# Transposing the exponential's rows as they are, and applying each head's reciprocal sum to its projected output

## The chip, the cores and the metric

The kernel runs on one core of one Trainium2 chip. The metric is device time in microseconds (us), the median of three runs; lower is better. The engines are named as the profile names them: PE is the tensor engine (matrix products), PEld its weight loads, ACT the scalar engine (exponentials), DVE the vector engine, POOL the gpsimd engine and SP the sync engine, which here issues most of the transfers. SBUF is the core's on-chip memory, PSUM the small memory that PE writes its products to.

## The reference

A block with two halves shares one conditioning vector. The first half, where the change lies, is attention of 2048 query rows over a cache of 2048 keys, with 32 query heads in 8 groups of 4 heads that share one key and value head:

```python
q = (h @ wq).reshape(B, Sq, 32, 128).transpose(0, 2, 1, 3)
scores = einsum('bhqd,bhkd->bhqk', q, k) * 128 ** -0.5      # k, v repeated 4 times per key head
p = softmax(scores, axis=-1)
o = einsum('bhqk,bhkd->bhqd', p, v)
x = x + ga * (o.transpose(0, 2, 1, 3).reshape(B, Sq, 4096) @ wo)
h = layernorm(x) * (1 + cb) + sb                            # then the second half
```

The second half is a gated spatial mixing block: `z = gelu(h @ w_in)`, the half `z2` of it normalised per row, multiplied from the left by a 2048 by 2048 matrix, a bias added, multiplied by the half `z1`, and projected by `w_out`. Data is bfloat16, sums are float32.

## The kernel before

**Units and iterations.** Work is cut into 128 units `u`: key head `g = u // 16` and query tile `j = u % 16` of 128 rows, with the 4 heads of the group in one unit. The main loop (L1373) has one iteration `it` for each unit and six more at the end; each has 8 slots `i`. The order of instructions on every engine is the order in which this loop writes them (a manual schedule): in each slot first what was put down for it with `at(it, slot, fn)`, then the scores and the exponential of unit `it` (`qk`), a share of the product with V of an earlier unit (`pv_part`), the query projection of a later block (`fill`), and at most one step of an output projection (`wo_proj`). From iteration 128 on each slot also takes three matmuls of the second half (`zrun(3)`).

**Two kinds of unit.** `by_rows(u)` is true for the even units from 8 to 124, 59 in all. In the other units the scores are computed with keys on the partitions, so the exponential comes out in the layout that the product with V needs; the row sums come from a column of ones beside V, and `pv` divides by them with a reciprocal and a multiplication (L1091, L1092) on a 128 by 256 piece. In a row unit the scores have queries on the partitions (L1005), ACT writes the exponential into a row buffer `pn` (the page names such a buffer `win_sb`, `wmod_a` or `pn`, since they share memory) and gives the sum of each half row (L1012). One head takes two slots. Two slots after its last exponential was written down, `turn_rows` adds the two half sums (L1045), takes the reciprocal into `rall` (L1048), multiplies the 128 by 2048 rows by it in place (L1050), and has a transfer of SP turn them (L1051). The product with V follows three iterations later (`pv_rows`, L1059), one 128 by 512 bank for four heads, which DVE copies to `oT` (L1068).

**Output projection.** `wo_proj(u)` makes four steps, one per head. Before, all four add up in one PSUM bank named `misc` (L1112), and DVE adds the bank to the unit's running sum `xacc` in SBUF (L1125; for the first key head it copies it, L1123). There are two `misc` banks, handed out in turn, and a matmul that opens a bank waits until DVE has read what stood there two turns earlier; the query projection (L945, read by DVE in L956) takes banks from the same two. For the last key head (units 112 to 127) four more DVE operations follow in a row: times `ga` (L1130), plus `x` (L1131), and the statistics of the second layer norm (L697, L698). I call these four the closing steps.

**Where the steps of a projection stand.** `wo_at(u)` puts the projection of a row unit 6 iterations after `u`, and that of another unit 4 after it; for units from 122 on it is one less. With four steps these take slots 4 to 7. Two iterations hold two projections, and there the eight steps fill slots 0 to 7: iteration 126 (units 120 and 123) and iteration 129 (units 124 and 126). In both the row unit comes first.

**The end.** After the last closing steps come, through `ln2`, one normalised tile each (L686), a transfer that turns it (L1149) and a scaling (L1156), then on DVE the statistics of `z2` (L1312, L1313) and its normalisation, which the spatial matmuls (L1456) read.

Of the kernel before, what the change touches and what calls it, by code (L numbers as in the profile page):

```python
# [11 lines left out]
FP32 = mybir.dt.float32  # L12
ACT = mybir.ActivationFunctionType
ALU = mybir.AluOpType
AX = mybir.AxisListType
P = 128
# [559 lines left out]
def kernel(  # L576
# [19 lines left out]
    nc = tc.nc  # L596
    _, S, D = A_x.shape
    _, HKV, SK, DH = A_k_cache.shape
    HQ = A_wq.shape[1] // DH
    REP = HQ // HKV  # L600
# [12 lines left out]
    NSLOT = NKT // 2  # L613
# [30 lines left out]
    late = free_b.enter_context(tc.tile_pool(name="late", bufs=2, side="right"))  # L644
    early = free_a.enter_context(tc.tile_pool(name="early", bufs=2))

    x_sb = res.tile([P, NT, D], BF16, name="x_sb")
    ga_rows = res.tile([P, D], FP32, name="ga_rows")
    gb_rows = res.tile([P, D], FP32, name="gb_rows")
    modc = res.tile([P, 6 * NDT], FP32, name="modc")  # L650
    rall = res.tile([P, NT * HQ], FP32, name="rall")
    mv1 = res.tile([P, NT, nc.vector.BN_AGGR_DIM], FP32, name="mv1")
    mv2 = res.tile([P, NT, nc.vector.BN_AGGR_DIM], FP32, name="mv2")
# [6 lines left out]
    pn = [win_t[:, r * SK : (r + 1) * SK] for r in range(REP - 1)]  # L660
# [34 lines left out]
    def ln_stats(mv, j, src):  # L695
        st = stat.tile([P, 1, nc.vector.BN_STATS_DIM], FP32, name="bnst")
        nc.vector.bn_stats(out=st[:, 0, :], in_=src)  # L697
        nc.vector.bn_aggr(out=mv[:, j, :], in_=st[:])  # L698
# [201 lines left out]
    for k in range(2):  # L900
        for dt in (2 * k, 2 * k + 1):
# [3 lines left out]
            else:  # L905
                nc.scalar.activation(
                    out=dst,
                    in_=src,
                    func=ACT.Identity,
                    scale=modc[:, NDT + dt : NDT + dt + 1],  # L910
# [52 lines left out]
    NU = HKV * NT  # L963


    TURN_A, TURN_B = 2 * CT, NU - 2

    def by_rows(u):
        return TURN_A <= u < TURN_B and u % 2 == 0

    def pv_at(u):
        return u + 3 if by_rows(u) else u + 1

    def wo_at(u):
        return pv_at(u) + (3 if u < TURN_B - CT else 2)
# [11 lines left out]
    def at(it, slot, fn):  # L987
        later.setdefault((it, slot), []).append(fn)

    def qk(u, i):  # L990
        g, j = divmod(u, NT)
        b, jj = g * NCH + j // CT, j % CT
        if i == 0:
            if homes[u] == "wsp":
                pTs[u] = wspp.tile([P, NT, 512], BF16, name="wsp")
            else:
                pTs[u] = late.tile([P, NKT, 512], BF16, name=homes[u], bufs=1)
            if by_rows(u):
                rsums[u] = stat.tile([P, NSLOT], FP32, name="rs")
        s_ps = bank2()  # L1000
        if by_rows(u):
            hh, half = divmod(i, 2)
            for c in range(2):
                k0 = (2 * half + c) * 512
                nc.tensor.matmul(  # L1005
                    s_ps[:, c * 512 : (c + 1) * 512],
                    lhsT=qTs[b][:, hh, jj * P : (jj + 1) * P],
                    rhs=groups[g]["kT"][:, k0 : k0 + 512],
                    start=True,
                    stop=True,  # L1010
                )
            nc.scalar.activation(  # L1012
                out=rows_of(u, hh)[:, half * HK : (half + 1) * HK],
                in_=s_ps[:],
                func=ACT.Exp,
                scale=inv_sqrt_dh,
                accum_out=rsums[u][:, i : i + 1],
            )
            if half == 1:
                at(*divmod(u * NSLOT + i + 2, NSLOT), lambda: turn_rows(u, hh))  # L1020
            return
        for h in range(2):
            kt = 2 * i + h
            nc.tensor.matmul(  # L1024
                s_ps[:, h * 512 : (h + 1) * 512].rearrange("p (r q) -> p r q", r=REP),
                lhsT=groups[g]["kT"][:, kt * P : (kt + 1) * P],
                rhs=qTs[b][:, :, jj * P : (jj + 1) * P],
                start=True,
                stop=True,
            )  # L1030
        nc.scalar.activation(  # L1031
            out=pTs[u][:, 2 * i : 2 * i + 2, :],
            in_=s_ps[:].rearrange("p (k q) -> p k q", k=2),
            func=ACT.Exp,
            scale=inv_sqrt_dh,
        )

    def rows_of(u, hh):
        return pn[((u - TURN_A) // 2 * REP + hh) % len(pn)][:, 0:SK]

    def turn_rows(u, hh):
        c0 = u * REP + hh
        rs, rinv = rsums[u], rall[:, c0 : c0 + 1]
        tot = stat.tile([P, 1], FP32, name="tot")
        nc.vector.tensor_tensor(  # L1045
            out=tot[:], in0=rs[:, 2 * hh : 2 * hh + 1], in1=rs[:, 2 * hh + 1 : 2 * hh + 2], op=ALU.add
        )
        nc.vector.reciprocal(out=rinv, in_=tot[:])  # L1048
        rows = rows_of(u, hh)
        nc.vector.tensor_scalar(out=rows, in0=rows, scalar1=rinv, scalar2=None, op0=ALU.mult)  # L1050
        nc.sync.dma_start_transpose(out=pTs[u][:, :, hh * P : (hh + 1) * P], in_=rows)  # L1051

    def pv_rows(u, i, n):

# [48 lines left out]

    def wo_proj(u):
        g, j = divmod(u, NT)
        ps = {}

        def mm(hh):
            if hh == 0:
                ps[0] = bank("misc")  # L1110
            X_ps = ps[0]
            nc.tensor.matmul(  # L1112
                X_ps[:],
                lhsT=oTs[u][:, hh, :],
                rhs=groups[g]["wo"][:, hh, :],
                start=(hh == 0),
                stop=(hh == REP - 1),
            )
            if hh < REP - 1:
                return  # L1120
            if g == 0:
                xaccs[j] = late.tile([P, D], FP32, name=f"xacc{j}", bufs=1)
                nc.vector.tensor_copy(out=xaccs[j][:], in_=X_ps[:])  # L1123
            else:
                nc.vector.tensor_tensor(  # L1125
                    out=xaccs[j][:], in0=X_ps[:], in1=xaccs[j][:], op=ALU.add
                )
            if g == HKV - 1:
                xa = xaccs[j]
                nc.vector.tensor_tensor(out=xa[:], in0=xa[:], in1=ga_rows[:], op=ALU.mult)  # L1130
                nc.vector.tensor_tensor(  # L1131
                    out=x_sb[:, j, :], in0=xa[:], in1=x_sb[:, j, :], op=ALU.add
                )
                ln_stats(mv2, j, x_sb[:, j, :])

        return [lambda hh=hh: mm(hh) for hh in range(REP)]

# [127 lines left out]
    for g in range(1, HKV):  # L1265
        it = (g - 1) * NT
        at(it + 11, 5, lambda g=g: load_k(g))
        loads = (
            lambda g=g: load_v(g),
            lambda g=g: load_wq(g, nc.gpsimd),  # L1270
            lambda g=g: load_wo(g, nc.gpsimd),
        )
        for k, load in enumerate(loads):
            if g == 1:
                at(5, 0, load)
                continue
            u = next(u for u in range(it + 4 + 2 * k, NU) if by_rows(u))
            at(u + 1, 5, lambda u=u: after_rows(u))
            at(u + 1, 5, load)

# [92 lines left out]
    for it in range(NU + 6):  # L1373
        if it < NU:
            if it % CT == 0 and it // CT + 1 < NB:
                set_fill(it // CT + 1)
        elif it == NU:
            free_a.close()
            z2p = fast.enter_context(tc.tile_pool(name="z2p", bufs=1))
            zs["z2"] = z2p.tile([P, NT, FH], BF16, name="z2")  # L1380
        pvs = [u for u in (it - 5, it - 3, it - 1) if 0 <= u < NU and pv_at(u) == it]
        wos = [u for u in range(max(it - 6, 0), min(it - 2, NU)) if wo_at(u) == it]
        wf = [fn for u in wos for fn in wo_proj(u)]
        for i in range(NSLOT):
            for fn in later.pop((it, i), []):
                fn()
            if it < NU:
                qk(it, i)
            if len(pvs) == 1:
                pv_part(pvs[0], i, NSLOT)  # L1390
            elif pvs:
                n = NSLOT // 2
                pv_part(pvs[i // n], i % n, n)
            for fn in fill.pop((it, i), []):
                fn()
            if i >= NSLOT - len(wf):
                wf[i - NSLOT + len(wf)]()
            if it >= NU:
                zrun(3)
        for u in wos:  # L1400
            if u >= (HKV - 1) * NT:
                ln2(it, u % NT)
        if it == NU + 2:
            free_b.close()
            mlp = fast.enter_context(tc.tile_pool(name="mlp", bufs=1, side="right"))
            zs["z1T"] = mlp.tile([P, NFT, S], BF16, name="z1T")
            wout_sb = mlp.tile([P, NFT, D], BF16, name="wout_sb")
            bsp_bc = mlp.tile([P, S], BF16, name="bsp_bc")
            nc.gpsimd.dma_start(out=wout_sb[:], in_=wout_dram)
            nc.gpsimd.dma_start(out=bsp_bc[:], in_=B_b_sp.partition_broadcast(P))  # L1410
# [165 lines left out]
```

## Time and profile before

| what | us |
|---|---|
| median of 3 runs (lowest, highest) | 1313.21 (1313.07, 1313.99) |
| span of the profiled execution, first to last instruction | 1311.5 |
| PE busy | 1303.8 |
| ACT busy | 1113.0 |
| DVE busy | 689.5 |
| POOL busy | 59.4 |
| rows times the reciprocal (L1050), 236 operations | 177.9 |
| bank added to `xacc` (L1125), 112 operations, and copied (L1123), 16 | 76.2 and 10.9 |

The page and the answers of the trace list, for each group of instructions, its line, engine and operation, the tile written and the tiles read, the shapes, the count, the busy time and the mean of one in nanoseconds, and after a bar the time that the engine stood idle just before them with what ended it. In a timeline the first two numbers are the start and the length in us, both on the span's clock. A matmul's length there includes the time in which its result travels; the next one starts earlier.

### The profile page before, as it was taken

Reading aid. Unit: us, or ns where it says so; the run is one execution under the profiler, and the core shown is the slowest. Engines: PE = TensorE matmul, PEld = TensorE weight load, DVE = VectorE, ACT = ScalarE, POOL = GpSimd, SP = SyncE. Lnnn points to the kernel's source line nnn. Section 1 sums busy time; section 2 is a strip of 40 time slices with the busy share of each in tenths; the row PEclk is TensorE's granted clock in tenths of the full one; section 3 lists DMA queues with packets and bytes.
Section 4 is the critical chain, followed back from the end, with each engine's and each line's share of the span. In section 5 each row is a group of like instructions: output and inputs, shape, how many; then the busy total and the mean of one; then the engine's idle time right before and its main releaser. Section 6 shows DMA issues by size and latency. Waiting matters only on the chain.

```text
span 1311.5 us, 24369 instructions
## 1 busy us (share of the span) xinstructions
PE 1303.8 (99%) x9527; PEld 736.9 (56%) x9527; DVE 689.5 (53%) x1693; ACT 1113.0 (85%) x1533; POOL 59.4 (5%) x115
## 2 busy tenths in 40 slices
PE   9999999999999999999999999999999999999998
PEld 5665555555555555555555555555555555644445
DVE  5644455444454544444445454444445588784444
ACT  7899999999999999999999999999999999550000
POOL 1200000000000000000000000000000011120000
PEclk9999999999999999999999999999999999999999
DMA  6669778877897677867886778668876688364300
GB/s 181 154 97 157 130 128 154 158 118 133 158 166 149 121 144 155 144 125 140 160 169 122 133 157 156 125 127 153 175 143 125 118 140 144 103 133 96 82 21 27
DMA packets 607723, 174.45 MB, mean 133 GB/s; under 512 B 597264, under 2 KB 603664, under 8 KB 607600
## 3 DMA queue, kind: packets, MB, share of 16 engines
q1 hardware_dynamic: 600576, 153.67, 64.9%
q0 software_dynamic: 4432, 16.91, 4.1%
q10 hardware_dynamic: 2592, 2.23, 0.5%
q8 instruction: 77, 1.26, 0.4%
q14 instruction: 46, 0.38, 0.1%
HBM read 21.89 MB, written 2.10 MB: 18 GB/s over the span
## 4 chain that ended last, share of the span: by engine, by line
PE 96%; DVE 2%; DMA 1%; POOL 0%; issue 0%; ACT 0%; DVEq 0%; POOLq 0%
PE o_ps L1080 19%; PE s_ps L1024 18%; PE s_ps L1005 16%; PE o_ps L1059 16%; PE misc L1112 8%; PE misc L945 8%; PE misc L1456 7%; PE s_ps L1290 1%; PE o_ps L1477 1%; DVE stz L1312 1%; PE s_ps L1477 1%; DMA xnT<-xn 0%; DMA wmod_a<-in_w_mod_dram 0%; DVE z L686 0%; POOL rstd_lnz L682 0%; PE misc L855 0%
## 5 line engine op out<-in xcount | busy, mean ns | idle before, releaser
L1031 ACT ACTIVATE pT<-s_ps 128x1024 bf16<-128x1024 f32 x552 | 561.1, 1025 | 30.7 <-PE s_ps L1024 8.7
L1080 PEld LDWEIGHTS <-pT 128*128 128x128 bf16 x4416 | 295.3, 98 | 128.9
L1080 PE MATMUL o_ps<-v,pT 128*128 128x129 bf16 x4416 | 339.7, 220 | 0.0
L1024 PE MATMUL s_ps<-qT,kT 128*128 128x512 bf16 x1104 | 328.1, 379 | 0.3 <-ACT pT L1031 0.2
L1005 PE MATMUL s_ps<-kT,qT 128*128 128x512 bf16 x944 | 280.7, 379 | 0.0
L1012 ACT ACTIVATE win_sb<-s_ps 128x1024 bf16<-128x1024 f32 x238 | 243.7, 1025 | 3.5
L1112 PE MATMUL misc<-wo_g,oT 128*128 128x512 bf16 x512 | 194.0, 379 | 0.0
L945 PE MATMUL misc<-hT,wq_g 128*128 128x512 bf16 (+2 forms) x520 | 187.0, 371 | 0.1
L1024 PEld LDWEIGHTS <-kT 128*128 128x128 bf16 x1104 | 107.3, 98 | 114.9 <-issue 2.3
L1012 ACT ACTIVATE pn<-s_ps 128x1024 bf16<-128x1024 f32 x156 | 159.6, 1024 | 2.0 <-ACT wmod_a L1012 0.3
L1059 PEld LDWEIGHTS <-v 128*128 128x128 bf16 x944 | 92.4, 98 | 111.4
L956 DVE CAST qT<-misc 128x512 bf16<-128x512 f32 x125 | 85.7, 686 | 122.8 <-PE misc L945 122.8
L1068 DVE CAST oT<-o_ps 128x512 bf16<-128x512 f32 x59 | 40.8, 692 | 194.9 <-PE o_ps L1059 194.9
L1059 PE MATMUL o_ps<-wsp,v 128*128 128x512 bf16 x480 | 142.1, 379 | 0.0
L1059 PE MATMUL o_ps<-pT,v 128*128 128x512 bf16 x464 | 138.0, 379 | 0.0
L1005 PEld LDWEIGHTS <-qT 128*128 128x128 bf16 x944 | 92.2, 98 | 61.6
L1045 DVE TENSOR_TENSOR tot<-rs 128x1 f32<-128x1 f32 x236 | 36.4, 154 | 127.1 <-ACT win_sb L1012 84.8
L1456 PE MATMUL misc<-wsp,z 128*128 128x512 bf16 (+2 forms) x560 | 101.4, 336 | 0.2
L1050 DVE TENSOR_SCALAR win_sb<-win_sb,rall 128x2048 bf16<-128x2048 bf16 x119 | 89.7, 753 | 4.4 <-DVE rall L1048 0.3
L1012 ACT ACTIVATE wmod_a<-s_ps 128x1024 bf16<-128x1024 f32 x78 | 79.9, 1025 | 0.0
L1456 PEld LDWEIGHTS <-z 128*128 128x128 bf16 x560 | 50.5, 98 | 49.4 <-DVE z L686 1.6
L1125 DVE TENSOR_TENSOR xacc<-misc,xacc 128x512 f32<-128x512 f32 x112 | 76.2, 680 | 0.0
(110 smaller groups left out, 824.1 us busy)
## 6 DMA issues: line engine op xcount, KB each, us to landing
v<-in_A_v_cache_dram POOLq DMA_DIRECT2D x7, 512.0 KB, 6.6
wq_g<-in_A_wq_dram POOLq DMA_DIRECT2D x7, 512.0 KB, 3.9
wo_g<-in_A_wo_dram POOLq DMA_DIRECT2D x7, 512.0 KB, 4.5
wsp<-in_w_mod_dram POOLq DMA_DIRECT2D x1, 2048.0 KB, 9.1
out_dram<-yout ACTq DMA_DIRECT2D x16, 128.0 KB, 1.7
win_sb<-in_B_w_in_dram POOLq DMA_DIRECT2D x1, 1792.0 KB, 8.0
x_sb<-in_A_x_dram SPq DMA_DIRECT2D x3, 512.0 KB, 6.1
oT<-onorm SPq DMA_TRANSPOSE x69, 2.8
```

The costliest lines, as they stand in the source:

```text
L945: nc.tensor.matmul(ps[0][:, o0 : o0 + n], lhsT=wqs[g][:, dt, hh * DH : (hh + 1) * DH], rhs=hTs[ch][:, dt, c0 : c0 + n], start=(dt == 0), s ...
L956: nc.vector.tensor_copy(out=dst, in_=src)
L1005: nc.tensor.matmul(s_ps[:, c * 512 : (c + 1) * 512], lhsT=qTs[b][:, hh, jj * P : (jj + 1) * P], rhs=groups[g]["kT"][:, k0 : k0 + 512], sta ...
L1012: nc.scalar.activation(out=rows_of(u, hh)[:, half * HK : (half + 1) * HK], in_=s_ps[:], func=ACT.Exp, scale=inv_sqrt_dh, accum_out=rsums[u ...
L1024: nc.tensor.matmul(s_ps[:, h * 512 : (h + 1) * 512].rearrange("p (r q) -> p r q", r=REP), lhsT=groups[g]["kT"][:, kt * P : (kt + 1) * P], ...
L1031: nc.scalar.activation(out=pTs[u][:, 2 * i : 2 * i + 2, :], in_=s_ps[:].rearrange("p (k q) -> p k q", k=2), func=ACT.Exp, scale=inv_sqrt_dh,)
L1050: nc.vector.tensor_scalar(out=rows, in0=rows, scalar1=rinv, scalar2=None, op0=ALU.mult)
L1059: nc.tensor.matmul(o_pss[u][:], lhsT=groups[g]["v1"][:, kt, 0:DH], rhs=pTs[u][:, kt, :], start=(kt == 0), stop=(kt == NKT - 1),)
L1080: nc.tensor.matmul(o_ps[:, hh % 2, 0 : DH + 1], lhsT=pTs[u][:, kt, hh * P : (hh + 1) * P], rhs=groups[g]["v1"][:, kt, 0 : DH + 1], start=( ...
L1112: nc.tensor.matmul(X_ps[:], lhsT=oTs[u][:, hh, :], rhs=groups[g]["wo"][:, hh, :], start=(hh == 0), stop=(hh == REP - 1),)
L1125: nc.vector.tensor_tensor(out=xaccs[j][:], in0=X_ps[:], in1=xaccs[j][:], op=ALU.add)
L1456: nc.tensor.matmul(g_ps[:, :n], lhsT=z2[:, st, f * P : (f + 1) * P], rhs=wsp[t][:, st, c0 : c0 + n], start=(st == 0), stop=(st == NT - 1 a ...
```

## The change

In a row unit the rows are no longer multiplied by the reciprocal. `turn_rows` issues the transposing transfer first, straight from the exponential, one slot earlier than before, and then adds the half sums and takes the reciprocal as before. The product with V is then short of the factor, and so is `oT`. `wo_proj` makes up for it: for a row unit each head's step opens a bank of its own, and DVE multiplies the bank by the head's column of `rall` while it adds it to `xacc`. Units that are not row units keep one bank and one addition. The order in which units, lags and buffers are chosen is written in another form and comes out the same.

```diff
     def turn_rows(u, hh):
         c0 = u * REP + hh
-        rs, rinv = rsums[u], rall[:, c0 : c0 + 1]
+        rs = rsums[u]
+        nc.sync.dma_start_transpose(
+            out=pTs[u][:, :, hh * P : (hh + 1) * P], in_=rows_of(u, hh)
+        )
         tot = stat.tile([P, 1], FP32, name="tot")
         nc.vector.tensor_tensor(
             out=tot[:], in0=rs[:, 2 * hh : 2 * hh + 1], in1=rs[:, 2 * hh + 1 : 2 * hh + 2], op=ALU.add
         )
-        nc.vector.reciprocal(out=rinv, in_=tot[:])
-        rows = rows_of(u, hh)
-        nc.vector.tensor_scalar(out=rows, in0=rows, scalar1=rinv, scalar2=None, op0=ALU.mult)
-        nc.sync.dma_start_transpose(out=pTs[u][:, :, hh * P : (hh + 1) * P], in_=rows)
+        nc.vector.reciprocal(out=rall[:, c0 : c0 + 1], in_=tot[:])
...
             if half == 1:
-                at(*divmod(u * NSLOT + i + 2, NSLOT), lambda: turn_rows(u, hh))
+                at(*divmod(u * NSLOT + i + 1, NSLOT), lambda: turn_rows(u, hh))
...
     def wo_proj(u):
         g, j = divmod(u, NT)
+        each = by_rows(u)
         ps = {}
 
+        def into(first, X_ps, scale):
+            if first:
+                xaccs[j] = late.tile([P, D], FP32, name=f"xacc{j}", bufs=1)
+            xa = xaccs[j]
+            if scale is None and first:
+                nc.vector.tensor_copy(out=xa[:], in_=X_ps[:])
+            elif scale is None:
+                nc.vector.tensor_tensor(out=xa[:], in0=X_ps[:], in1=xa[:], op=ALU.add)
+            elif first:
+                nc.vector.tensor_scalar(
+                    out=xa[:], in0=X_ps[:], scalar1=scale, scalar2=None, op0=ALU.mult
+                )
+            else:
+                nc.vector.scalar_tensor_tensor(
+                    out=xa[:], in0=X_ps[:], scalar=scale, in1=xa[:], op0=ALU.mult, op1=ALU.add
+                )
+
         def mm(hh):
-            if hh == 0:
+            if hh == 0 or each:
                 ps[0] = bank("misc")
...
             nc.tensor.matmul(
...
-                start=(hh == 0),
-                stop=(hh == REP - 1),
+                start=(hh == 0 or each),
+                stop=(hh == REP - 1 or each),
             )
+            if each:
+                c0 = u * REP + hh
+                into(g == 0 and hh == 0, ps[0], rall[:, c0 : c0 + 1])
+            elif hh == REP - 1:
+                into(g == 0, ps[0], None)
-            if hh < REP - 1:
+            if hh < REP - 1 or g < HKV - 1:
                 return
...
```

The closing steps for the last key head are unchanged. In the built program PE, ACT, POOL and SP carry the same instructions in the same order as before; on DVE 236 multiplications of rows go and 177 operations on banks come.

More of the change, by code (lines that the diff above doesn't have):

```diff
@@ L966 @@
     TURN_A, TURN_B = 2 * CT, NU - 2
+    LAGS = (3, 1)
     def by_rows(u):
-        return TURN_A <= u < TURN_B and u % 2 == 0
+        return TURN_A <= u < TURN_B and (u - TURN_A) % len(LAGS) < len(LAGS) - 1
+    row_units = [u for u in range(NU) if by_rows(u)]
     def pv_at(u):
-        return u + 3 if by_rows(u) else u + 1
+        return u + (LAGS[(u - TURN_A) % len(LAGS)] if by_rows(u) else 1)
     def wo_at(u):
@@ L1038, in rows_of @@
     def rows_of(u, hh):
-        return pn[((u - TURN_A) // 2 * REP + hh) % len(pn)][:, 0:SK]
+        return pn[(row_units.index(u) * REP + hh) % len(pn)][:, 0:SK]
     def turn_rows(u, hh):
         c0 = u * REP + hh
-        rs, rinv = rsums[u], rall[:, c0 : c0 + 1]
+        rs = rsums[u]
+        nc.sync.dma_start_transpose(
+            out=pTs[u][:, :, hh * P : (hh + 1) * P], in_=rows_of(u, hh)
+        )
         tot = stat.tile([P, 1], FP32, name="tot")
@@ L1108, in mm @@
         def mm(hh):
-            if hh == 0:
+            if hh == 0 or each:
                 ps[0] = bank("misc")
-            X_ps = ps[0]
             nc.tensor.matmul(
-                X_ps[:],
+                ps[0][:],
                 lhsT=oTs[u][:, hh, :],
                 rhs=groups[g]["wo"][:, hh, :],
-                start=(hh == 0),
-                stop=(hh == REP - 1),
-            )
-            if hh < REP - 1:
-                return
[L1121 to L1134, printed above, removed]
+                start=(hh == 0 or each),
+                stop=(hh == REP - 1 or each),
+            )
+            if each:
[3 more added lines that the diff above has]
+                into(g == 0, ps[0], None)
@@ L1136, in wo_proj @@
+            if hh < REP - 1 or g < HKV - 1:
+                return
+            xa = xaccs[j]
+            nc.vector.tensor_tensor(out=xa[:], in0=xa[:], in1=ga_rows[:], op=ALU.mult)
+            nc.vector.tensor_tensor(
+                out=x_sb[:, j, :], in0=xa[:], in1=x_sb[:, j, :], op=ALU.add
+            )
+            ln_stats(mv2, j, x_sb[:, j, :])
         return [lambda hh=hh: mm(hh) for hh in range(REP)]
@@ L1276 @@
                 continue
-            u = next(u for u in range(it + 4 + 2 * k, NU) if by_rows(u))
+            u = next(u for u in range(it + 4 + 2 * k, NU) if by_rows(u) and not by_rows(u + 1))
             at(u + 1, 5, lambda u=u: after_rows(u))
@@ L1380 @@
             zs["z2"] = z2p.tile([P, NT, FH], BF16, name="z2")
-        pvs = [u for u in (it - 5, it - 3, it - 1) if 0 <= u < NU and pv_at(u) == it]
-        wos = [u for u in range(max(it - 6, 0), min(it - 2, NU)) if wo_at(u) == it]
+        pvs = [u for u in range(max(it - 5, 0), min(it, NU)) if pv_at(u) == it]
+        wos = [u for u in range(max(it - 8, 0), min(it, NU)) if wo_at(u) == it]
         wf = [fn for u in wos for fn in wo_proj(u)]
```

## The prediction

> **What bounds the kernel now.** I read the page's engine and chain parts first, then the stages, then the timeline in the middle and at the two places where the change meets a full queue.
>
> ```profile
> span 1311.5 us, 24369 instructions
> PE 1303.8 (99%) x9527; PEld 736.9 (56%) x9527; DVE 689.5 (53%) x1693; ACT 1113.0 (85%) x1533; POOL 59.4 (5%) x115
> ...
> PE 96%; DVE 2%; DMA 1%; POOL 0%; issue 0%; ACT 0%; DVEq 0%; POOLq 0%
> ```
>
> PE is the chain. The stages (each stretch's length, then the busy time of PE, PEld, DVE, ACT and POOL, and last granted clock, DMA share and GB/s) say how completely:
>
> ```profile
> 122.00:1091.00 969.00, 969.00 (x7092) 548.60 (x7091) 489.19 (x1213) 945.08 (x1331) 27.80 (x54) 1.00 0.77 143
> 1126.00:1186.00 60.00, 59.79 (x338) 30.24 (x337) 51.11 (x130) 30.41 (x32) 11.56 (x20) 1.00 0.52 103
> ```
>
> From 122 to 1091 us PE is busy for 969.00 of 969.00 us at full granted clock. In the timeline there, matmuls of 512 columns start 0.216 us apart whatever stands around them, so nothing waits. From 1126 to 1186 us DVE is busy 51.11 of 60 us: the one stage where it is nearly as full as PE. The costliest DVE groups that the change touches, kept apart by shape:
>
> ```profile
> L1050 DVE TENSOR_SCALAR win_sb<-win_sb,rall 128x2048 bf16<-128x2048 bf16 x119 | 89.7, 753 | 4.4 <-DVE rall L1048 0.3
> L1125 DVE TENSOR_TENSOR xacc<-misc,xacc 128x512 f32<-128x512 f32 x112 | 76.2, 680 | 0.0
> ```
>
> **The change, part by part.** *Removed:* 236 row multiplications of 0.753 us, 177.7 us of DVE (0.753 is the mean of the largest of the three groups of L1050). PE did not wait for them: the product with V comes three iterations later, some 26 us, and a turning transfer lands in 4.3 to 4.7 us. Gain on the path: 0. *Moved:* the transposes are issued one slot (1.1 us) earlier and wait for ACT alone; their order on SP among the oT transposes and key loads, the POOL queue, ACT's and PE's orders are the same as before, so nothing is overtaken. Rows come free earlier; ACT stood idle 5.5 us in all ahead of the row exponentials (L1012), and none of it reached PE in the middle. Gain 0. If that cover were gone, PE would wait for landings, and it would show at L1059, where it now waits for nothing. The half sums now stand one slot earlier on DVE and may hold what is behind them until the exponential ends; that is included below.
>
> *Added:* 59 units by 3 more DVE operations on a bank, 177, and three more waits of PE per row unit, since every step now opens a bank. No row shows this operation (bank times a column plus `xacc`). Nearest is L1125, which reads the same bank and the same `xacc`: 0.68 us. Below it lies 0.41 us (L686, 512 elements from SBUF); above it a multiplication and an addition one after the other, 0.69 + 0.68 = 1.37. I take 0.68. DVE's balance is then 177.7 - 177 x 0.68 = 57 us less. A matmul whose wait is already met costs nothing: the first steps of L1112 and L945 carry such a wait now and start 0.216 us after their predecessor like all others.
>
> *The banks in the middle.* A row iteration, on the timeline from 601.38 us: the query bank is read by 606.99, the second step opens it at 607.76, margin 0.77 us. The half sums end at 607.25; the first bank is read from 607.29 to 607.97 and the third step needs it at 608.87, margin 0.9. The second bank is free at 608.86, the fourth step comes at 609.97, margin 1.1; the third is free at 609.97, and the next query projection takes it at 611.05. No wait. In the last key head (rows read in iterations 118 to 124) `xn` and `hT`, 0.41 and 0.98 us, stand between the reads and use the margins up to about 0.2 us: still none.
>
> *The banks in iteration 126.* Here the eight steps begin in slot 0, and DVE is still in the closing steps of unit 121:
>
> ```profile
> 1106.41 0.68 DVE L1125 TENSOR_TENSOR xacc<-misc,xacc 128x512 f32<-128x512 f32 x1
> ...
> 1109.31 0.18 DVE L698 BATCH_NORM_AGGREGATE mv<-bnst 128x2 f32<-128x6 f32 x1
> ```
> ```profile
> 1106.70 0.38 PE L1112 MATMUL misc<-wo_g,oT 128*128 128x512 bf16 x1
> ...
> 1107.80 0.38 PE L1112 MATMUL misc<-wo_g,oT 128*128 128x512 bf16 x1
> ...
> 1108.90 0.38 PE L1112 MATMUL misc<-wo_g,oT 128*128 128x512 bf16 x1
> ```
>
> Before, these steps shared one bank and none waited. Now the first opens one bank, the second the other (free since 1107.1), and the third, at 1108.90, needs the first bank read. DVE reaches that read at 1109.41 (an operation that does not need the aggregate starts 0.10 after it, as at 1137.91 to 1138.01) and ends at 1110.09. PE waits 1.2 us, and scores, V products and exponentials of the iteration wait behind it. PE is gapless from here to 1183 us, so this is not made up.
>
> *The banks in iteration 129.* The same with the closing steps of unit 125 ahead, and slots only 0.78 us long:
>
> ```profile
> 1137.91 0.18 DVE L698 BATCH_NORM_AGGREGATE mv<-bnst 128x2 f32<-128x6 f32 x1
> 1138.01 0.66 DVE L1125 TENSOR_TENSOR xacc<-misc,xacc 128x512 f32<-128x512 f32 x1
> ```
> ```profile
> 1135.05 0.38 PE L1112 MATMUL misc<-wo_g,oT 128*128 128x512 bf16 x1
> ...
> 1136.62 0.38 PE L1112 MATMUL misc<-wo_g,oT 128*128 128x512 bf16 x1
> ```
>
> The first bank of unit 124 is read from 1138.01 to 1138.69; the third step wants it at 1136.62. PE waits 2.07 us. Unit 122, in iteration 127, has its steps 1.55 us apart and its reads in DVE's idle time: no wait.
>
> *What DVE hands on.* From 1134.46 to 1160.7 us DVE has no idle time, and through the last tile's transfer and the `z2` statistics it leads to the first spatial matmuls:
>
> ```profile
> 1164.70 0.98 DVE L1156 TENSOR_SCALAR hT<-xnT,modc 128x128 bf16<-128x128 bf16 x4 [3.98 <-DMA xnT<-xn]
> ...
> 1183.77 1.78 DVE L686 TENSOR_SCALAR z<-z,mvz,rstd_lnz 128x896 bf16<-128x896 bf16 x4 [1.47 <-POOL rstd_lnz L682]
> ```
> ```profile
> 1181.48 8.83 PE L1456 MATMUL misc<-wsp,z 128*128 128x512 bf16 x36
> ```
>
> 36 matmuls at 0.216 us and 0.16 for the last to finish are 7.93 us, so PE waits 0.9 us there now. Unit 124's three more reads follow each other 0.71 us apart (as L1130 follows L1125): DVE is later by 2.13 + 1.2 = 3.33 us, PE by 1.2 + 2.07 = 3.27, and the wait grows by 0.06.
>
> **Sum:** 1.2 + 2.07 + 0.06 = 3.3 us; the span 1311.5 becomes 1314.8. The median of the runs lies 1.7 us above the profiled span; on it, 1313.2 + 3.3 = **1316.5 us**. With 0.41 us per read each wait is 0.27 shorter and the sum 2.8; with 0.75 it is 3.4. From about 0.8 us the margins of 0.2 in the last head are spent, and at 1.37 every row unit waits: reads and half sums between the second step and the next query bank are then 1.37 + 0.35 + 1.37 behind the first read's end at 608.66, that is 611.75 against 611.05, 0.7 us for 58 units, some 41 us.
>
> The Trainium skill, VectorE: DVE Perf Modes, section Rules for kernel authors, speaks against the change: fusing buys nothing on chained vector operations, one should lower their count. Taken alone it would price the bank operations as 177 more, 120 us of DVE by the row of 0.68; the trace agrees with the count, but only the two places above put it on PE's path.
>
> **Rivals.** *The chain to the spatial matmuls has slack (not slower by what can be told).* The last tile's transfer takes 6.1 us from issue to landing, where the median of the 16 is 3.0. If the shift takes it out of the crowd of loads around 1155 us, the closing statistics come up to 3.1 us earlier against PE, and from 0.9 us on PE's present wait is gone: 3.3 - 0.9 = 2.4, 1315.6 us. For it: DVE's idle 3.98 us before it. Against: the loads that crowd it wait for the same DVE chain and shift too.
>
> *Only one wait comes.* If DVE is ahead in iteration 126 by the removed multiplications, 2.1 us remain: 1315.3. Against: the closing steps there wait for PE's product (oT ends at 1106.49), not for DVE.
>
> *The reads are dear.* Between 0.8 and 1.37 us: 1317 to 1358. Against: L1125 and all other 512-element bank reads are 0.68 to 0.69.
>
> *The clock falls in the longer wait.* At the start of the trace ten 512-column matmuls take 4.29 us, 0.43 each, twice the later pace; 4 us at half pace lose 2: 1318.5. Against: PE waited 0.9 us at 1184 and kept its pace. The Trainium skill, TensorE: Matmul & The Clock Gate, Part 1: The HAM clock gate, wants an idle window of about 3.4 us for a fall; no run here shows one, and both waits are shorter.
>
> *A gain.* All there is to win is the 0.9 us at 1184 and some ten row slots between 83 and 122 us that the chain shows stretched by 0.1 us: 2 us, 1311.2. Against: the former follow ACT's pace, 1.10 us a row slot, which stays.
>
> **How the numbers follow.** Forecast 0.58, slack 0.14, one wait 0.10, dear reads 0.08, clock 0.06, gain 0.04. About 0.2% (2.6 us) can be told from no change. Slower is then 0.52 of the forecast with dear reads and clock, 0.66; the rest of the forecast, slack, one wait and most of the gain are within it, 0.31; faster 0.03. The range runs from 1314.4, a us below the slack and one-wait cases, to 1318.6, which takes in the clock; below it the gain, above it the dear reads are left out, with some error in the forecast itself.
>
> **What would show it.** Right: third steps of L1112's successor waiting for DVE about 1.2 us near 1109 and 2.1 near 1138, no other PE wait that is new, reads near 0.68 us, L1050 gone, and the spatial matmuls about 3.3 us later. Wrong: PE waits in the middle stage, reads above 0.8 us, or gaplessness in both iterations.

## The result and the profile after

| | before | after |
|---|---|---|
| median of five runs beside one another, us | 1313.07 | 1318.35 |
| lowest and highest, us | 1312.90 and 1313.99 | 1316.17 and 1319.82 |
| ratio after to before | | 1.0036, 95% interval 1.0024 to 1.0048 |
| profiled execution: span, us | 1311.5 | 1314.1 (the execution of 1316.17) |

The change makes the kernel slower: its shortest run lies 2.2 us above the longest of the kernel before. The execution that was profiled is the shortest of the five; the last experiment looks at others. First the page of the kernel after, its span, its engines and the engine shares of its chain:

```profile
span 1314.1 us, 23878 instructions
PE 1303.4 (99%) x9527; PEld 737.0 (56%) x9527; DVE 637.2 (48%) x1634; ACT 1112.4 (85%) x1533; POOL 54.6 (4%) x115
...
PE 98%; DVE 1%; ACT 0%; issue 0%; DVEq 0%
```

DVE is busy for 52 us less than before, and the span is 2.6 us longer. The work that went was not on the chain. The stages, in the columns used for the kernel before (length, busy time of PE, PEld, DVE, ACT and POOL with counts, granted clock, DMA share, GB/s):

```profile
122.00:1091.00 969.00, 969.00 (x7098) 548.84 (x7097) 439.44 (x1157) 944.57 (x1333) 24.79 (x54) 1.00 0.80 143
...
1126.00:1186.00 60.00, 58.00 (x344) 30.06 (x341) 52.81 (x132) 31.30 (x32) 11.12 (x20) 1.00 0.44 99
```

In the middle PE is busy in all of the 969 us, as before, with 50 us less on DVE beside it. The last stage holds 2 us of idle PE and a DVE that is 1.7 us busier. What PE waited for there (a row of the view of waits: total, times, longest) and the price of the new operation (a row of the groups by shape):

```profile
PE misc L1133 <- DVE xacc L1126: 3.1, 2, 2.0
```
```profile
L1126 DVE SCALAR_TENSOR_TENSOR xacc<-misc,rall,xacc 128x512 f32<-128x512 f32 x232 | 172.5, 744 | 20.0 <-PE misc L1133 14.9
```

Two waits, 3.1 us. The timeline shows where they stand. Iteration 126:

```profile
1107.44 0.38 PE L1133 MATMUL misc<-wo_g,oT 128*128 128x512 bf16 x1
...
1108.95 0.18 DVE L698 BATCH_NORM_AGGREGATE mv<-bnst 128x2 f32<-128x6 f32 x1
...
1109.05 2.43 DVE L1126 SCALAR_TENSOR_TENSOR xacc<-misc,rall,xacc 128x512 f32<-128x512 f32 x3
...
1109.82 0.38 PE L1133 MATMUL misc<-wo_g,oT 128*128 128x512 bf16 x1 [1.11 <-DVE xacc L1126]
```

Iteration 129:

```profile
1136.75 0.38 PE L1133 MATMUL misc<-wo_g,oT 128*128 128x512 bf16 x1
...
1138.82 0.18 DVE L698 BATCH_NORM_AGGREGATE mv<-bnst 128x2 f32<-128x6 f32 x1
...
1138.92 3.28 DVE L1126 SCALAR_TENSOR_TENSOR xacc<-misc,rall,xacc 128x512 f32<-128x512 f32 x4
...
1139.69 0.38 PE L1133 MATMUL misc<-wo_g,oT 128*128 128x512 bf16 x1 [2.00 <-DVE xacc L1126]
```

In both, the aggregate that closes the statistics of units 121 and 125 ends, the first read starts 0.10 us after the aggregate did, and the matmul that needs that bank starts 0.77 us later. The idle time in brackets begins at the modelled end of the matmul before. Counted from start to start, and less the usual pace, PE lost 1.275 us in iteration 126 and 2.165 us in iteration 129, and 0.07 us more at each of two later steps of iteration 129: 3.6 us in all. Further on, some time came back:

```profile
1165.78 0.98 DVE L1174 TENSOR_SCALAR hT<-xnT,modc 128x128 bf16<-128x128 bf16 x4 [1.53 <-DMA xnT<-xn]
...
1184.69 1.78 DVE L686 TENSOR_SCALAR z<-z,mvz,rstd_lnz 128x896 bf16<-128x896 bf16 x4 [1.47 <-POOL rstd_lnz L682]
```

```profile
1184.70 15.49 PE L1474 MATMUL misc<-wsp,z 128*128 128x512 bf16 x71
```

DVE waited 1.53 us for the last tile's transfer, where it waited 3.98 before, and PE's 0.9 us wait ahead of the spatial matmuls is gone: 71 matmuls at 0.216 us and 0.16 for the last to finish are the 15.49 us. With 0.35 us less at the start of this execution: 3.6 - 0.9 - 0.35 = 2.35 of the 2.6 us between the two spans.

### The profile page after: what moved, and what is told of

Its sections match the earlier page's. It is cut to its first block, busy times and chain, and to the rows that moved or that the text cites. A ratio compares the mean times of both kernels' runs of the same rounds, so it can differ in the third digit from the quotient of the medians.

```text
span 1314.1 us, 23878 instructions
## 1 busy us (share of the span) xinstructions
PE 1303.4 (99%) x9527; PEld 737.0 (56%) x9527; DVE 637.2 (48%) x1634; ACT 1112.4 (85%) x1533; POOL 54.6 (4%) x115
## 4 chain that ended last, share of the span: by engine, by line
PE 98%; DVE 1%; ACT 0%; issue 0%; DVEq 0%
PE o_ps L1084 19%; PE s_ps L1028 18%; PE s_ps L1009 16%; PE o_ps L1063 16%; PE misc L1133 8%; PE misc L945 8%; PE misc L1474 7%; PE s_ps L1347 2%; PE s_ps L1308 2%; PE o_ps L1495 1%; PE s_ps L1495 1%; PE o_ps L786 0%; PE misc L855 0%; PE o_ps L945 0%; DVE hT L814 0%; DVE bnst L697 0%
## 5 line engine op out<-in xcount | busy, mean ns | idle before, releaser
L1126 DVE SCALAR_TENSOR_TENSOR xacc<-misc,rall,xacc 128x512 f32<-128x512 f32 x232 | 172.5, 744 | 20.0 <-PE misc L1133 14.9
L1095 DVE RECIPROCAL rall<-o_ps 128x2 f32<-128x2 f32 x138 | 23.5, 170 | 98.2 <-PE o_ps L1084 91.1
```

The costliest lines, as they stand in the source:

```text
L1126: nc.vector.scalar_tensor_tensor(out=xa[:], in0=X_ps[:], scalar=scale, in1=xa[:], op0=ALU.mult, op1=ALU.add)
```

## The experiments

Every kernel below was run beside the kernel before. The kernel before had medians of 1313.1 to 1314.5 us in these comparisons, so the ratios, or the distances from the kernel before, are what compares. Line numbers of edited kernels are a few higher than those of the kernel after.

### The change taken back for single units

For the units named in `OLD`, which is `(120, 124)`, `(124,)` or `(120,)`, rows are multiplied and turned as before the change, and one bank is filled and read once. Two lines of the edit:

```diff
+    OLD = (120, 124)
...
-        each = by_rows(u)
+        each = by_rows(u) and u not in OLD
```

Units 120 and 124:

> Units 120 and 124 alone go the old way (rows multiplied before the transfer, one bank, one addition); the other 57 row units keep the change. Theory A (all of the loss is made where these two units' banks wait, in iterations 126 and 129, directly or through what those waits do to the clock): no PE wait of L1133's successor, every execution at clock 0.999, 1312.2 to 1313.4 us, that is 0 or a little less than before. Rival B (the spread and the lower mean clock of the changed kernel come from something the change does everywhere, such as denser transfers or the unnormalised rows): median 1315 or more, executions at 0.998 remain.

Unit 124 alone:

> Unit 124 alone goes the old way, so the wait of about 1.3 us in iteration 126 stays and that of 2.2 us in iteration 129 goes. Theory A: 1313.1 + 1.3 less up to 0.9 given back ahead of the spatial matmuls, 1313.5 to 1314.5 us, little spread, no execution at 0.998. Rival B: as the changed kernel, 1316 to 1320 with spread.

Unit 120 alone:

> Unit 120 alone goes the old way, so only the wait of about 2.2 us in iteration 129 stays. Theory A: 1314.2 to 1315.4 us where the clock holds, and some 2 us more where it falls (some executions at 0.998); median 1315 to 1317. Rival B: no different from the changed kernel less 1.3 us, and no tie between the long times and this wait.

| taken back for | ratio to before, 95% interval | waits of PE on `xacc` in its trace |
|---|---|---|
| 120 and 124 | 1.0013, 1.0004 to 1.0022 | 0.7 us in iteration 120, 1.0 us in iteration 124 |
| 124 | 1.0012, 1.0003 to 1.0021 | 0.7 us in iteration 124, 1.2 us in iteration 126 |
| 120 | 1.0027, 1.0017 to 1.0037 | 0.7 us in iteration 120, 2.0 us in iteration 129 |
| none (the kernel after, in the comparison of the result) | 1.0036, 1.0024 to 1.0048 | 1.1 us in iteration 126, 2.0 us in iteration 129 |

The wait of a unit that is taken back goes, and that of the other stays within 0.1 us. But each of these kernels brought a wait of its own, so none returned to the time before: the four row multiplications of 0.75 us of unit 120 or 124 fall into iterations in which the bank reads of units 114 or 118 stand, and there is no room for both. That is the mix of old and new work, which neither of the two kernels has. In time, theory A holds for unit 120 alone (2.9 us over the kernel before), is 0.3 us short for unit 124 (1.7 where it had at most 1.4), and fails for both units together, where it had no loss and 2.1 us came; there the median is as rival B had it. Since the new waits explain that as well, these runs do not decide between the two. As an undo they are not clean, and they say only that in the last key head some 0.75 us more on DVE in an iteration is already a wait.

### The change taken back for the whole last head

```diff
+    OLD = (112, 114, 116, 118, 120, 122, 124)
```

> The change is taken back for the units from 112 on alone (their rows are multiplied ahead of the turn, and a unit fills one bank), and kept for the 52 row units 8 to 110. Theory A: the middle costs nothing, so the time is that of the kernel before, within 0.6 us, and the profiled trace has no wait of TensorE on xacc above 0.3 us. Rival C (four reads of 744 ns in place of one of 680 cost in the middle too): at least 1.5 us over the kernel before, with waits on xacc spread over the middle.

1313.66 us against 1313.80, ratio 1.0001 (0.9992 to 1.0010). No wait on `xacc` is left in the view of waits. The largest row is one wait near 85 us, ahead of the middle stage:

```profile
PE s_ps L1010 <- ACT win_sb L1017: 1.8, 1, 1.8
```

So the change is free in 52 of its 59 units, and the whole loss comes from the last key head. This is the cleanest result of the study.

### Free banks for unit 124

The third and fourth step of unit 124 open banks of another pool, which is free at that time, so that they need not wait for the first reads:

```diff
-                ps[0] = bank("misc")
+                ps[0] = bank("o_ps" if u == 124 and hh >= 2 else "misc")
```

> The changed kernel, with the last two steps of unit 124 in banks of o_ps, which are free then, so that no matmul of iteration 129 waits for DVE; DVE's three more operations there stay. If the wait in iteration 129 is all of its price: 1314 us (only the 1.3 us of iteration 126 are left) and no execution at 0.998. If DVE's queue decides up to the spatial matmuls: the 2.1 us come back there as four shorter waits, 1315.3 to 1316.5 us, and the clock holds since no single wait is long.

1317.55 us, ratio 1.0025 (1.0015 to 1.0034). The wait of 2.0 us fell to 0.43 us at the step that followed, and the time hardly moved: 3.5 us over the kernel before, near what was expected if DVE's queue decides (2.2 to 3.4 us over). Its rows of waits say why:

```profile
PE misc L1133 <- DVE xacc L1126: 1.5, 2, 1.1
...
PE s_ps L1347 <- ACT z1T L1355: 1.0, 1, 1.0
```

The second row is new: 1 us at 1158.85 us, some 18 us further on, for an evacuation by ACT. The next experiment shows what that waits for.

### The same work in another order

The closing steps of units 121 and 125 are issued behind the four reads of units 120 and 124, and the two small steps of the normalisation that need them a few slots later. Nothing is added or left out (the main lines of the edit; `close` holds the closing steps):

```diff
+    LATE = (121, 125)
...
+            if u in LATE:
+                at(wo_at(u) + 1, 4, close)
+            else:
+                close()
+
+        def close():
             xa = xaccs[j]
...
+        at(it + 1, 4 if late_j else 0, first)
+        at(it + 1, 7 if late_j else 4, second)
```

> The changed kernel, but the closing steps of units 121 and 125 (gate, sum into x, statistics) are issued behind the four reads of units 120 and 124 in iterations 126 and 129, and the two small steps that need them a few slots later. The same VectorE work in another order. Theory A (what costs is that four reads stand behind closing steps): both waits are gone (under 0.3 us each), the time is 2.5 to 4 us under the changed kernel, that is 0.9 us under to 0.7 us over the kernel before. Rival E (the VectorE work of the last head is too much in any order, as the spare banks suggested, and the loss comes back further on): the waits go, but the time stays at 1.5 to 3 us over the kernel before, with new idle time ahead of the spatial matmuls or in iterations 127 to 133.

1315.94 us, ratio 1.0017 (1.0008 to 1.0026). The two waits are gone, as both theories had it: no row of the view of waits has `xacc`. The time is rival E's. Of the 4.9 us that the kernel after was over the kernel before in the same comparison, 2.1 stay. The timeline of this kernel shows where:

```profile
1155.40 0.69 DVE L1156 TENSOR_TENSOR x_sb<-xacc,x_sb 128x512 bf16<-128x512 f32 x1
...
1156.25 1.94 ACT L1363 ACTIVATE z1T<-s_ps 128x1024 bf16<-128x1024 f32 x2 [2.90 <-DVE x_sb L1156]
...
1157.33 1.02 PE L1355 MATMUL s_ps<-hT,win_sb 128*128 128x512 bf16 x4 [1.47 <-ACT z1T L1363]
```

ACT may not write `z1T` until DVE has closed the last tile (L1156 adds it into `x_sb`, and it is the last reader of `xacc`); `z1T` is placed once the attention's tiles are given up. ACT stood 2.90 us, its banks stayed full, and PE waited 1.47 us. In the kernel before the same two lines read:

```profile
1151.90 0.69 DVE L1131 TENSOR_TENSOR x_sb<-xacc,x_sb 128x512 bf16<-128x512 f32 x1
...
1153.23 1.02 ACT L1337 ACTIVATE z1T<-s_ps 128x1024 bf16<-128x1024 f32 x1 [0.86 <-PE s_ps L1329]
```

There DVE was done at 1152.59 us, 0.64 us ahead of ACT, which waited for PE. So behind the two waits on banks lies a second bound: the length of DVE's own queue in the last head. The kernel after does not show it, because its PE and ACT come to this place 3.2 us later than before (`z1T` at 1156.45 us, 0.32 us behind DVE). With the waits on banks taken away they come early again, and DVE, which has the same additional work as in the kernel after, has not closed the last tile. The spare banks gave the same: 2.42 us of ACT ended by `x_sb`, and 1 us of PE.

In this trace (span 1313.7 us) the new wait costs 1.64 us from start to start, the 0.9 us ahead of the spatial matmuls are given back, and 1.1 us of a wait for weights near 48 us, which other executions have too, make up most of the rest of the 2.2 us.

### A longer wait

Three more multiplications of 0.69 us, on values that nothing reads any more, are put behind the closing steps of unit 125:

```diff
+            if u == 125:
+                for _ in range(3):
+                    nc.vector.tensor_tensor(out=xa[:], in0=xa[:], in1=ga_rows[:], op=ALU.mult)
```

> The changed kernel with three more multiplications of xacc of unit 125 (some 0.69 us each, on values that nothing reads any more) behind its closing steps, so ahead of the reads of unit 124. Theory A: the wait in iteration 129 grows from 2.0 to 4.1 us idle, and the time by 2.1 us over the changed kernel, matmuls behind the wait at their usual 0.19 to 0.21 us. Rival D (TensorE idle for long enough loses its clock): the matmuls behind the wait take twice that for some 3 us or more in the trace, the granted clock falls there, and the time grows by 3.5 to 5.5 us.

1321.25 us, ratio 1.0052 (1.0038 to 1.0066), 2.5 us over the kernel after in the same comparison. The wait became 4.05 us, as both theories had it. Then the timeline shows the clock of rival D:

```profile
1143.32 0.58 PE L1133 MATMUL misc<-wo_g,oT 128*128 128x512 bf16 x1 [4.05 <-DVE xacc L1126]
1143.70 1.32 PE L1311 MATMUL s_ps<-win_sb,hT 128*128 128x448 bf16 x3
...
1146.44 1.51 PE L1311 MATMUL s_ps<-win_sb,hT 128*128 128x448 bf16 x6
```

Three matmuls of 448 columns take 1.32 us at first, and six take 1.51 us three microseconds later. The stretches in between say it with the granted clock (third value from the end):

```profile
1143.30:1146.10 2.80, 2.78 (x8) 1.09 (x8) 2.11 (x3) 0.92 (x1) 0.00 (x0) 0.50 0.21 47
1146.20:1149.00 2.80, 2.75 (x15) 1.39 (x15) 2.66 (x7) 0.92 (x1) 0.27 (x1) 1.00 0.00 0
```

Eight matmuls in place of fifteen in 2.8 us: some 1.5 us lost on top of the wait. Of the 5.1 us of this profile over the profile after, 2.05 us are the longer wait, 1.5 the clock, 1.2 a wait for weights near 48 us, and the rest some tenths at the start. In the medians the growth of 2.5 us lies nearer to theory A's 2.1 than to the 3.5 to 5.5 of rival D, though the one trace shows D at work. The medians cannot separate the two if some executions of the kernel after lose the clock as well, which is taken up in the last experiment.

### Reads of double length in the middle

Every bank of a row unit is read twice by the same instruction in the heads ahead of the last:

```diff
+                if g < HKV - 1:
+                    into(False, ps[0], rall[:, c0 : c0 + 1])
```

> The changed kernel with every read of a bank of a row unit done twice, by the same instruction, in the heads ahead of the last one (so the products of these units are added twice there). A bank is then held 1.5 us instead of 0.74 in 52 row units; the last head is as in the changed kernel. Theory A (the middle is free only for as long as a bank is read within its margin of 0.77 to 1.1 us, and at 1.4 us a row unit waits 0.7 us): waits of TensorE on xacc in every row unit of the middle, together 35 to 60 us, and the time as much longer. Rival F (what counts in the middle is the sum of VectorE's work, which has room: 439 us busy of 969, and 155 us more still fit): waits of less than 5 us in all.

1372.98 us, ratio 1.0454 (1.0423 to 1.0484). Its waits:

```profile
PE misc L945 <- DVE xacc L1126: 23.9, 52, 0.5
PE misc L1133 <- DVE xacc L1126: 16.7, 54, 2.0
```

52 waits at the next query projection and 52 at a third or fourth step (the other two are those of iterations 126 and 129). From start to start they cost 0.62 and 0.42 us a unit: 1.04 x 52 = 54 us. The spans lie 57.0 us apart (1371.1 and 1314.1): 1.0 us more is a wait for the exponentials near 85 us, 1.5 us are lost to the clock in iteration 129 (shown in the last experiment), and the rest is the start. So theory A holds, and rival F does not. DVE is busy for 597 of 1038 us in that stretch. It has room in the sum and none at the place.

### The kernel after, once more

> The changed kernel once more, on the chip that runs the three kernels beside it. Both theories: the two waits of TensorE on the reads of xacc stand where they stood, 1.1 us idle in iteration 126 and 2.0 us in iteration 129, and the profiled span is 1314 to 1317.5 us. Theory A (the two waits, less what the shorter landing of the last tile gives back ahead of the spatial matmuls, are all of the loss): 2 to 3.5 us over the kernel before, its executions within 1.5 us of one another but for what the kernel before spreads too. Rival D (after the 2 us wait the granted clock falls in some executions): executions of 4 to 6 us over the kernel before among them, and where the profiled one is of these, matmuls of twice their usual time behind the wait in iteration 129.

> The changed kernel, one profile, to see one of the longer executions. Both theories: waits of 1.1 and 2.0 us in iterations 126 and 129. Rival D (the clock falls behind the 2 us wait in some executions): where the mean granted clock is 0.998, matmuls behind the wait in iteration 129 at 0.37 us for 448 columns in place of 0.19, for some 3 us. Rival G (what makes an execution longer lies elsewhere: the wait on the exponentials at 85 us, the loads at 47 us, the wait ahead of the spatial matmuls, as in the trace of 1318.8 us): the matmuls behind the wait keep their pace.

> The same, a second profile: as for the first. Theory A with rival G: span 1314 plus what the waits at 47, 85 and 1190 us add in this execution. Rival D: 1.5 to 2 us more than that sum, with the fallen clock behind one of the two waits.

> The changed kernel a last time, to see one of the longer executions in a trace. Rival D (the clock falls behind the 2 us wait in some executions): matmuls of 448 columns at 0.37 us behind the wait in iteration 129 where the execution takes over 1318 us. Rival G (the rest lies in waits elsewhere that vary from execution to execution): the two waits of 1.1 and 2.0 us, no slower matmuls behind them, and the span is 1314 plus what the other waits add. Either way the executions lie between 1316 and 1321 us.

The two comparisons of several runs gave 1.0032 (1.0020 to 1.0044) and 1.0031 (1.0019 to 1.0042). With the first, five executions were profiled, and the two waits are the same in all: 1.27 and 2.16 to 2.17 us from start to start. No matmul behind them is slow in these five. What differs lies elsewhere:

| span, us | what else PE waited for |
|---|---|
| 1314.1 | nothing to speak of |
| 1314.8 | 0.6 us more in the first 25 us |
| 1315.6 | 0.8 us for weights at 48 us, 0.6 us more in the first 25 us |
| 1315.8 | 0.9 us for the exponentials at 85 us, 0.65 us more in the first 25 us |
| 1318.8 | 2.2 us for the exponentials at 85 us, 0.7 us for weights at 48 us, 0.2 us more in the first 25 us, 1.6 us in and ahead of the first spatial matmuls |

The longest of them, in its rows of waits:

```profile
PE misc L1133 <- DVE xacc L1126: 3.1, 2, 2.0
PE s_ps L1009 <- ACT win_sb L1016: 2.1, 1, 2.1
...
PE misc L1474 <- DVE z L686: 0.8, 1, 0.8
```

So rival G holds for these five executions. The last row says that the time given back ahead of the spatial matmuls is not given back in each execution: here DVE waited 4.35 us for the last tile's transfer.

Rival D is not out, though. The kernel with the double reads has the last head of the kernel after, with the same wait of 2.00 us in iteration 129, and in its trace the clock falls behind that wait:

```profile
1195.24 0.38 PE L1133 MATMUL misc<-wo_g,oT 128*128 128x512 bf16 x1 [2.00 <-DVE xacc L1126]
...
1196.64 1.32 PE L1310 MATMUL s_ps<-win_sb,hT 128*128 128x448 bf16 x3
```
```profile
1195.80:1199.20 3.40, 3.40 (x11) 1.32 (x9) 3.12 (x5) 0.92 (x1) 0.00 (x0) 0.50 0.34 77
1199.20:1202.60 3.40, 3.40 (x19) 1.69 (x18) 3.30 (x12) 1.69 (x2) 0.85 (x2) 1.00 0.19 39
```

Three matmuls of 448 columns take 1.32 us, and eleven matmuls stand in 3.4 us where nineteen follow. From the second step to the first run of fifteen matmuls PE takes 8.77 us here and 7.22 us in the kernel after, so the fall costs 1.55 us beyond the wait. The wait of 2.00 us stands in seven traces (the five, the undo of unit 120 alone, and this one), and the clock fell in one. The clock records suggest why. In both traces with a fall (this one and the longer wait) the clock is at 0.50 for 3.41 us, and the fall begins a whole number of such stretches after the clock first came up, 349 and 333. Counted in this way, the 2.00 us lie within one stretch here; in the other six traces the edge of a stretch cuts the wait, and at most 1.39 to 1.96 us lie on one side of it. That fits a clock that is set stretch by stretch, but it is one fall against six, with 1.96 us close to 2.00.

The untraced executions point the same way without showing it. The mean granted clock was 0.998 or 0.997 in 10 of the 20 executions of the kernel after, with a median of 1318.7 us, where the other ten have 1317.2; of 67 executions of the kernel before in these comparisons, one had 0.998. But the mean alone is no proof: in the trace of 1315.6 us it is 0.998 because the clock is at 0.50 from 1311.5 us on, after the last matmul.

## Why the prediction was right, step by step

*The middle costs nothing.* Right. PE has 969.00 of 969.00 us, and with the last head taken back the ratio is 1.0001. The margins of 0.77 to 1.1 us that carry this were tested too: reads of 1.5 us broke them in all 52 units and cost 54 us. The forecast had 0.7 us a unit for reads of 1.37 us; three operations of 0.12 us more make it 1.06, against 1.04 measured.

*The price of a read.* Mis-sized: 0.744 us, where 0.68 was taken. It lies between the bounds 0.41 and 1.37 and close to the row that was chosen. The multiplication inside the addition adds 0.064 us to a read, 15 us over 232 reads. By the groups, 177.9 + 76.2 + 10.9 us of multiplications, additions and copies before became 172.5 + 38.8 + 8.2 + 2.9, that is 42.6 us less, and not the 57 of the forecast. (The engine's own busy time fell by 52; it counts once what the records of neighbouring operations overlap, as the aggregate above and the read that starts 0.08 us before its end do.)

*The wait in iteration 126.* Forecast 1.2 us, measured 1.275. *The wait in iteration 129.* Forecast 2.07, measured 2.165 and twice 0.07. The excess is the longer read, 0.064 us in each, and some hundredths. Taking back unit 120 or 124 took away its wait and not the other. *Unit 122 in iteration 127* has no wait, as the forecast had it.

*What DVE hands on.* This step failed. It let the 0.9 us ahead of the spatial matmuls grow by 0.06; in four of the five traces it went instead, as the first rival said: the last tile's transfer came out of its crowd, and DVE waited 1.5 to 2.1 us for it in place of 3.98. In the fifth it stayed. The step also saw only one place at which DVE's queue reaches PE. There is another, 30 us earlier: the write to `z1T` waits for the closing of the last tile, with 0.64 us of slack in the kernel before. It cost the kernel after nothing, since PE was late already; it is why taking away the waits on banks returned a little over half of the loss.

*The sum.* The steps give 3.6 us as measured, less 0.9 for the wait that went: 2.7 us in the typical trace, against a forecast of 3.3. The medians of the three comparisons lie 5.3, 4.9 and 3.3 us over those of the kernel before. What is between, 0.6 to 2.6 us, is not wholly explained. In the traced executions it is the start and the waits at 48 and 85 us, ahead of the part that costs; but the kernel with the last head taken back shares that start (its trace has 1.8 us at 85 us) and still has the median of the kernel before. A fall of the clock behind the wait in iteration 129, 1.55 us where it was traced, is of the right size and place, but no trace of the kernel after has it. So the forecast, 1316.5 us, has the right mechanism at the right two places and has one wait too many in its sum, and what makes most executions longer than the traced steps stays open. That the median of the result, 1318.35 us, lies within the range owes something to luck: 1316.5 is 1.9 us too low, and the range's upper end was drawn for the clock's 1318.5, a case that was given a chance of 0.06.

*The clock.* Mis-sized as a rival. The sum put its cost at nothing and its chance at 0.06, since PE had kept its pace behind a wait of 0.9 us. In the five traces of the kernel after that holds: no matmul behind the waits of 1.1 and 2.0 us is slow. In the trace of the double reads the same 2.00 us were enough, and PE lost 1.55 us more, where the rival had 2; at 4.05 us the clock fell too. The Trainium skill, TensorE: Matmul & The Clock Gate, Part 1: The HAM clock gate, asks for an idle window of about 3.4 us, and says that the window runs freely. The traces do not bear out the first as the shortest wait that is dangerous, since 2.00 us of idle time were followed by a fall. They fit the second: both falls last 3.41 us, and the same wait brought a fall in one trace and none in six. Which of the untraced executions have a fallen clock could not be seen; it stays open.

*Only one wait; dear reads; a gain.* None came. Both waits are there in every trace of the kernel after, 0.744 us is below the 0.8 us from which reads are dear, and the row slots before 122 us kept their pace.

No kernel here is faster than the kernel before. PE has no idle time that the removed multiplications could have filled, so the version with the last head taken back is as good as can be shown, and equal.

## What to carry to other kernels

Count an operation that moves work from one long instruction to several short ones at the place where its buffer is needed next, not in the sum of its engine: here 52 us less of DVE made the kernel slower, and in the middle 0.74 us a bank were free where 1.5 us cost 54 us. Look for such places where the pattern ends, in the last head, where the work that is saved lies earlier than the work that is added and the closing steps stand in the same queue. And when a wait is taken away, ask what the same queue would hold up next, since a second bound can lie hidden right behind the first. Do not price a wait of PE by its length alone: 2.00 us cost 1.55 us more in one trace of seven, through the clock.

## What the runs showed of the hardware

- A fused multiplication and addition of 512 float32 elements from a bank and from `xacc` takes 0.744 us, and the addition alone 0.680 us.
- PE kept its clock through an idle time of 2.00 us in six traces and lost it after the same 2.00 us in a seventh, and after 4.05 us in another: the clock was at 0.50 for 3.41 us, some 1.5 us lost beyond the wait itself.
- The five traced executions of the kernel after differ by up to 4.7 us, of which waits near 48 and 85 us make up to 2.9 us. At 85 us, in the longest, ACT stood for 2.06 us. The cause of that was not found.
